# Two stores listed ahead of the last evictions, and twelve more idle products early on, in a fused mLSTM and feed-forward kernel

## The chip, the cores and the metric

One core of one Trainium2 chip runs the whole program as one launch. The metric is device time in microseconds (us). Smaller is better. Three runs of the kernel before gave 504.98, 501.16 and 502.6 us; the median is 502.6 us.

## The reference

The program computes two stages. The first is a gated recurrent attention (mLSTM) over 4 batches of 8 heads, 768 steps, head size 40. The second is a feed-forward layer with a rational activation over the 3072 resulting rows of 320 numbers.

```python
for t in range(S):
    m_new = np.maximum(f_gate[:, :, t] + m, i_gate[:, :, t])     # running maximum
    f_stab = np.exp(f_gate[:, :, t] + m - m_new)
    i_stab = np.exp(i_gate[:, :, t] - m_new)
    C = f_stab * C + i_stab * outer(vt, kt);  n = f_stab * n + i_stab * kt
    y[:, :, t] = sigmoid(o_gate[:, :, t]) * (C @ qt) / np.maximum(np.abs(n @ qt), 1.0)
h = x @ w_in                                  # x: y as 3072 x 320
P = a[0] + a[1] * h + a[2] * h**2 + a[3] * h**3
Q = 1.0 + np.abs(b[0]) * np.abs(h) + np.abs(b[1]) * h**2
out = (P / (Q + 1e-06)) @ w_out               # 3072 x 320
```

## The kernel before

**Work.** The recurrence is cut into chunks of 64 steps. A unit (`attention(u)`, u from 0 to 23) is one block of 128 steps of one batch; two units make one block of 256 rows for the feed-forward layer, so there are 12 such blocks. `feed_forward(n, i)` handles block n and hidden slice i (8 slices). Weights and activations are split into a high and a low part, and the parts are multiplied separately.

**Order.** Every operation is first put into a plan (`plan.add`) under a name such as `ev_11_7` (operation, block, slice). A second operation of the same name gets `.1`, a third `.2`. The text `ORDER` lists all names, and operations are issued in exactly that order. On one engine the listed order is therefore the order of execution. DMAs with the engine name `SP` are issued by SyncE in listed order; a DMA whose data is not ready holds up those behind it.

**Buffers.** `_Plan.issue` (line 122) chooses the physical buffer of a new tile when its first operation is issued: among the buffers of that kind it takes the one whose last user was issued the longest ago. A buffer with a user that has not been issued yet cannot be chosen. The framework then makes the new writer wait until the old readers of that buffer, stores included, have finished.

**The end.** The kind `ot` (line 1379), the staging tile of the output, has two buffers. The operation `ev` (`f_ev`, line 1378) copies a finished sum of 128 rows from PSUM into an `ot` tile; in the last block, `ev_11_7` is on ScalarE and `ev_11_7.1` on VectorE, and each also issues its own two stores, one on SyncE's queue and one on ScalarE's queue. For the earlier blocks the stores are an operation of their own, `ed` (`f_ed`, line 1395), with two stores on SyncE's queue. `ed_10_7` and `ed_10_7.1` store the two tiles of block 10.

```python
k = self.slot[tag] = min(range(bufs), key=free_since)       # line 132, _Plan.issue
...
ot = d["ot", t] = ring(fp, "ot", [P, DM], f"ot{n}_{t}")     # line 1379, f_ev
...
if last and not split:
    f_ed(t, (nc.scalar, nc.sync) if engine == "ACT" else (nc.sync, nc.scalar))
```

**The start.** `early()` (line 519) computes the running maximum and the exponentials of the first 256 steps on VectorE: the steps `early`, `early.1` and so on. `early.17` writes the exponentials into tile `g`; `early.18` (`turn`, line 551) is the only TensorE step of that list, a product with the identity that turns `g` (it writes tile `pe`). Behind it on TensorE stand `pf_0` (tile `fb`, 32 instructions), `pa_0` and `pa_1` (tile `pa`, 32 instructions each), which copy gate values across partitions, and `tk_0` (tile `kq`). ScalarE copies out what these write: `pc_0` and `pc_1` (tile `ab`), `ek_0` (tile `kT`), and after them prepares weights (`s2_o0`, `s0_o0`, and `o0_o1`, which writes tile `wo`). VectorE's `s1_o0` waits for `s0_o0`, its next step `o2_o1` reads what `o0_o1` wrote. GpSimd's `lx.1` is held until `o2_o1` is done, and the load `ogl_4` on SyncE's queue needs the buffer that `o2_o1` read last.

`busy()` (line 709) plans 90 operations `hot`: products of the identity with itself whose result nothing reads. Each is two instructions on TensorE. They are listed wherever TensorE would have nothing to do early in the program; the first 16 of them stand ahead of `early.18`. They read only the identity, so none of them waits for data of this stage.

Of the kernel before, what the change touches and what calls it, by code (L numbers as in the profile page):

```python
# [167 lines left out]
s0_o5.1 s2_o5 s2_i6 qa_0 hot.28 hot.29 hot.30 s1_o5.1 s0_o5 ow_0 tk_1 o0_o0 ke_1 s1_o5 ogl_2 ogl_0 s3_i6 s3_o5.1 u0_0
d1_0 ek_1 s3_o5 hot.31 hot.32 hot.33 hot.34 gate.7 gate.8 gate.9 gate.10 ogl_4 lq_1 tq_1 eq_1 lk_2 pf_2 u1_0 gate.11
qa_1 lv_1 o0_i4 o0_i6 kp_2 S_1 P_1 gate.12 P_1.1 pa_3 pc_3 ogl_5 sc_2 ogl_3 ow_1 u0_1 d1_1 gate.18 gate.13 gate.14  # L170
u1_1 gate.15 tk_2 ek_2 o2_i4 ogl_1 og_0 it_0 it_0.1 o2_i6 i1_0 gate.19 ke_2 hot.35 hot.36 hot.37 hot.38 hot.39 ab_0
ab_0.1 gate.16 raw_i0 lq_2 tq_2 rc_0 s0_i0 s2_i0 eq_2 o0_o5 s1_i0 s3_i0 o0_i0 g_0 x_0 g_0.1 hot.40 hot.41 hot.42
hot.43 raw_j1 s2_j1 qa_2 x_0.1 xd_0 S_2 P_2 P_2.1 lk_3 kp_3 o2_i0 pf_3 sc_3 o2_o0 s0_j1 s1_j1 raw_i1 xt_0 xh_0 xl_0
s2_i1 s0_i1 o2_o5 xh_0.1 xl_0.1 raw_i2 s0_i2 s2_i2 hot.44 hot.45 hot.46 s3_j1 ke_3 o0_j1 hot.47 hot.48 hot.49 hot.50
hot.51 hot.52 hot.53 hot.54 hot.55 f1_0_0 tk_3 ek_3 f1_0_0.1 ha_0_0 hot.56 hot.57 hot.58 s1_i1 lq_3 tq_3 gate.3 raw_o2
gate s3_i1 o0_i1 inverse squares gate.21 gate.17 hot.59 hot.60 hot.61 u_0_0 w_0_0 eq_3 o2_j1 s0_o2 hot.62 hot.63
hot.64 hot.65 hot.66 s1_i2 gate.20 s3_i2 s1_o2 p1_0_0 p3_0_0 S_3 gate.24 P_3 P_3.1 hot.67 hot.68 hot.69 hot.70 hot.71
hot.72 hot.73 s2_o2 s3_o2 o0_i2 raw_i3 s0_i3 s2_i3 lv_2 o2_i1 f1_0_1 f1_0_1.1 hot.74 hot.75 hot.76 hot.77 hot.78 s1_i3
s3_i3 y_0_0 r0_0_0 o2_j1.1 o2_i2 f1_0_2 f1_0_2.1 o0_i3 s0_o2.1 ha_0_1 u_0_1 p1_0_1 ha_0_2 u_0_2 w_0_1 w_0_2 lf_4 sc_4
gh_0_0 m_0_0 rm_0_0 s1_o2.1 p3_0_1 y_0_1 r0_0_1 gate.25 qa_3 hot.79 hot.80 hot.81 hot.82 hot.83 hot.84 hot.85 hot.86  # L180
hot.87 lk_4 gate.1 ow_2 u0_2 d1_2 gl_0_0 gh_0_1 m_0_1 rm_0_1 raw_o3 s2_o3 hot.88 hot.89 f2_0_0 lv_3 u1_2 s3_o2.1
p1_0_2 s0_o3.1 p3_0_2 ow_3 u0_3 s1_o3.1 raw_i5 ogl_6 d1_3 u1_3 o0_o2 it_1 it_1.1 i1_1 y_0_2 gl_0_1 s3_o3.1 s0_i5
f2_0_0.1 ab_1 ab_1.1 rc_1 raw_i7 o2_i3 lf_5 s0_i7 s2_i5 r0_0_2 kp_4 s1_i5 s1_i7 s2_i7 f1_0_3 f1_0_3.1 ha_0_3 g_1 g_1.1
f3_0_0 f3_0_0.1 o2_o2 p1_0_3 x_1 x_1.1 gh_0_2 xd_1 u_0_3 w_0_3 raw_o4 s0_o4.1 f2_0_1 f2_0_1.1 s3_i7 o0_i7 xt_1 xh_1
m_0_2 rm_0_2 p3_0_3 la_4 d0_4 lk_5 lq_4 xh_1.1 f3_0_1 f3_0_1.1 f2_0_2 f2_0_2.1 lq_5 s3_i5 o0_i5 tk_4 ke_4 kp_5 xl_1
xl_1.1 s1_o4.1 y_0_3 lv_4 s0_o4 gl_0_2 s2_o4 s3_o4.1 f1_1_0 f1_1_0.1 r0_0_3 gh_0_3 la_5 raw_o7 raw_o6 s1_o4 m_0_3 ek_4
s0_o3 s1_o3 ha_1_0 tq_4 eq_4 qa_4 s3_o3 s3_o4 f1_1_1 rm_0_3 gl_0_3 f1_1_1.1 f1_1_2 la_6 gate.33 lk_6 lv_5 p1_1_0
# [5 lines left out]
u_0_4 w_0_4 P_5.1 s1_o7 s3_o7 sc_6 gl_1_2 f1_0_5 ow_5 u0_5 kp_6 gate.31 ogl_9 la_7 gh_1_3 f1_0_5.1 ha_0_5 f1_0_6 lf_7
f1_0_6.1 s0_o6 s1_o6 u_0_5 d1_5 w_0_5 p1_0_4 p1_0_5 ha_0_6 f3_1_1.1 f2_1_2 f2_1_2.1 f3_1_2 m_1_3 s3_o6 u1_5 it_2
it_2.1 i1_2 gate.27 o0_o4 o2_o4 p3_0_4 rm_1_3 gl_1_3 ke_6 y_0_4 r0_0_4 gh_0_4 ab_2 ab_2.1 rc_2 g_2 g_2.1 tk_6 ek_6
p3_0_5 u_0_6 f3_1_2.1 f2_1_3 f2_1_3.1 m_0_4 rm_0_4 w_0_6 la_8 ogl_22 x_2 x_2.1 xd_2 y_0_5 r0_0_5 gh_0_5 f3_1_3
f3_1_3.1 tq_6 eq_6 lq_8 qa_6 gl_0_4 f1_0_7 f1_0_7.1 m_0_5 S_6 P_6 lk_8 p1_0_6 pe_1_3 pe_1_3.1 ha_0_7 s0_o6.1 p3_0_6
# [5 lines left out]
eq_7 f1_1_7 gate.22 gate.23 f1_1_7.1 f1_2_0 f1_2_0.1 gl_1_4 ha_1_7 ogl_11 ogl_7 gate.26 lv_7 lk_9 u_1_7 w_1_7 lf_8
ev_0_7.1 qa_7 gl_1_5 sc_7 ke_7 kp_8 ow_6 u0_6 d1_6 f2_1_4 f2_1_4.1 f3_1_4 lq_9 lk_10 ed_0_7 y_1_6 r0_1_6 p1_1_7 gh_1_6
ha_2_0 d0_7 u_2_0 og_6 S_7 P_7 P_7.1 p3_1_7 u1_6 sc_8 m_1_6 f3_1_4.1 f2_1_5 f2_1_5.1 f3_1_5 tk_8 ek_8 f3_1_5.1 f2_1_6
ow_7 u0_7 d1_7 w_2_0 p1_2_0 rm_1_6 gl_1_6 it_3 it_3.1 i1_3 tq_8 p3_2_0 u1_7 f2_1_6.1 f1_2_1 f3_1_6 f3_1_6.1 y_1_7
r0_1_7 gh_1_7 m_1_7 f1_2_1.1 d0_8 f2_1_7 ogl_14 f2_1_7.1 y_2_0 ab_3 ab_3.1 rc_3 g_3 g_3.1 r0_2_0 gh_2_0 rm_1_7 x_3
m_2_0 rm_2_0 gl_1_7 ha_2_1 p1_2_1 p3_2_1 u_2_1 eq_8 f1_2_2 f1_2_2.1 ha_2_2 p1_2_2 u_2_2 f3_1_7 x_3.1 gl_2_0 f3_1_7.1
ev_1_7 qa_8 ke_8 S_8 P_8 w_2_1 ogl_21 ed_0_7.1 p3_2_2 gate.29 ev_1_7.1 y_2_1 r0_2_1 gh_2_1 f1_2_3 kp_9 f1_2_3.1 ha_2_3
xd_3 xt_3 xh_3 w_2_2 m_2_1 y_2_2 u_2_3 r0_2_2 P_8.1 rm_2_1 w_2_3 f2_2_0 xl_3 f2_2_0.1 la_9 f3_2_0 f3_2_0.1 gh_2_2  # L210
p1_2_3 lq_10 p3_2_3 tk_9 ek_9 m_2_2 rm_2_2 f1_2_4 f1_2_4.1 f1_2_5 ha_2_4 gate.28 ogl_15 ogl_18 lf_9 sc_9 ke_9 kp_10
gl_2_1 y_2_3 r0_2_3 u_2_4 w_2_4 p1_2_4 xh_3.1 xl_3.1 gl_2_2 f1_2_5.1 ha_2_5 f2_2_1 f2_2_1.1 tq_9 eq_9 p1_2_5 f3_2_1
f3_2_1.1 f2_2_2 u_2_5 w_2_5 p3_2_4 gh_2_3 m_2_3 rm_2_3 y_2_4 r0_2_4 f2_2_2.1 f3_2_2 ogl_19 f3_2_2.1 f2_2_3 S_9 lk_11
lv_8 ogl_23 lv_9 lf_10 qa_9 P_9 P_9.1 gate.32 gh_2_4 m_2_4 ow_8 f1_2_6 f1_2_6.1 f1_2_7 f1_2_7.1 sc_10 u0_8 rm_2_4 d1_8
f2_2_3.1 gl_2_3 f3_2_3 f3_2_3.1 ha_2_6 u_2_6 w_2_6 p3_2_5 p1_2_6 u1_8 gl_2_4 ow_9 it_4 it_4.1 ed_1_7 y_2_5 d0_9 p3_2_6
u0_9 d1_9 u1_9 ha_2_7 u_2_7 w_2_7 r0_2_5 p1_2_7 gh_2_5 m_2_5 rm_2_5 p3_2_7 i1_4 ab_4 la_10 lq_11 lk_12 la_11 tk_10
ek_10 ke_10 ab_4.1 rc_4 g_4 kp_11 y_2_6 f2_2_4 f2_2_4.1 f1_3_0 gl_2_5 g_4.1 r0_2_6 gh_2_6 y_2_7 r0_2_7 m_2_6 rm_2_6
# [1308 lines left out]
```

## Time and profile before

| | |
|---|---|
| median of three runs | 502.6 us |
| profiled execution | 503.76 us, its span 502.0 us |
| mean granted TensorE clock | 0.985 of 2.4 GHz |
| TensorE busy | 479.1 us (95%) |
| VectorE, ScalarE, GpSimd busy | 418.6 us (83%), 400.0 us (80%), 380.2 us (76%) |
| chain that ended last, by engine | TensorE 82%, VectorE 9%, ScalarE 4%, DMA 2% |

The span is the time from the first to the last instruction of one profiled execution. "Busy" counts the time in which an engine executes something. The chain that ended last is followed back from the last instruction, at each step to what released it. A row with [3.77 <-DMA x] says that the engine sat idle for 3.77 us and that the DMA of x ended that wait. DMA issues are shown under SPq and ACTq, the queues of SyncE and ScalarE. The granted clock is given as a share of 2.4 GHz: 1.00 is that level, 0.50 is 1.2 GHz.

### The profile page before, as it was taken

Reading aid. Unit: us, or ns where it says so; the run is one execution under the profiler, and the core shown is the slowest. Engines: PE = TensorE matmul, PEld = TensorE weight load, DVE = VectorE, ACT = ScalarE, POOL = GpSimd, SP = SyncE. Lnnn points to the kernel's source line nnn. Section 1 sums busy time; section 2 is a strip of 40 time slices with the busy share of each in tenths; the row PEclk is TensorE's granted clock in tenths of the full one; section 3 lists DMA queues with packets and bytes.
Section 4 is the critical chain, followed back from the end, with each engine's and each line's share of the span. In section 5 each row is a group of like instructions: output and inputs, shape, how many; then the busy total and the mean of one; then the engine's idle time right before and its main releaser. Section 6 shows DMA issues by size and latency. Waiting matters only on the chain.

```text
span 502.0 us, 14204 instructions
## 1 busy us (share of the span) xinstructions
PE 479.1 (95%) x5631; PEld 462.8 (92%) x5631; DVE 418.6 (83%) x713; ACT 400.0 (80%) x696; POOL 380.2 (76%) x380
## 2 busy tenths in 40 slices
...
GB/s 200 187 165 235 209 172 158 103 79 69 118 120 123 94 93 27 150 84 24 66 69 79 68 82 2 74 80 64 2 117 27 21 76 3 37 5 2 14 0 47
DMA packets 119837, 42.01 MB, mean 84 GB/s; under 512 B 104274, under 2 KB 112530, under 8 KB 119762
## 3 DMA queue, kind: packets, MB, share of 16 engines
...
## 4 chain that ended last, share of the span: by engine, by line
PE 82%; DVE 9%; ACT 4%; DMA 2%; issue 1%; POOL 1%; SPq 1%; DVEq 0%; POOLq 0%; ACTq 0%
PE ph L34 34%; PE po L34 31%; PE kq L34 4%; PE y L34 4%; PE ow L34 3%; PE ps L34 3%; DVE w L34 2%; PE px L34 2%; DVE gH L34 1%; DVE gL L34 1%; PE hot L34 1%; DVE p L34 1%; PE pa L34 1%; PE fb L34 1%; DMA rawj<-in_moe_w_in_dram 1%
## 5 line engine op out<-in xcount | busy, mean ns | idle before, releaser
L34 PE MATMUL ph<-xk,wi 128*128 128x256 f32 x1152 | 169.8, 283 | 0.3 <-DVE na L34 0.3
L34 POOL TENSOR_TENSOR p<-p,w 128x512 f32<-128x512 f32 (+1 forms) x91 | 122.0, 1341 | 57.0 <-DVE w L34 52.5
L34 PEld LDWEIGHTS ph<-xk,wi 128*128 128x128 f32 x1152 | 148.1, 188 | 2.3 <-POOL wi L34 0.6
L34 POOL TENSOR_TENSOR w<-w,ha 128x512 f32<-128x512 f32 (+1 forms) x96 | 125.9, 1314 | 10.0 <-ACT w L34 6.1
L34 PE MATMUL po<-wo,gH 128*128 128x320 f32 x768 | 131.6, 310 | 0.0
L34 PEld LDWEIGHTS po<-wo,gH 128*128 128x128 f32 x768 | 115.4, 188 | 0.3
L34 DVE SCALAR_TENSOR_TENSOR w<-w,gH 128x512 f32<-128x512 f32 (+1 forms) x97 | 81.1, 837 | 4.2 <-DVE gH L34 0.5
L34 ACT ACTIVATE w<-ha,ba 128x512 f32<-128x512 f32 (+1 forms) x97 | 78.5, 811 | 6.0 <-POOL p L34 1.7
L34 DVE SCALAR_TENSOR_TENSOR gL<-p,ps,ph 128x512 fp32r<-128x512 f32 (+1 forms) x97 | 71.1, 734 | 14.3 <-POOL p L34 12.5
L34 DVE SCALAR_TENSOR_TENSOR gH<-p,ps,ph 128x512 fp32r<-128x512 f32 (+1 forms) x97 | 71.3, 735 | 12.6 <-ACT ph L34 9.1
L34 ACT ACTIVATE ph<-w,cd 128x512 f32<-128x512 f32 (+1 forms) x97 | 66.5, 687 | 16.3 <-DVE p L34 10.4
L34 ACT ACTIVATE ha<-ph 128x512 f32<-128x512 f32 (+1 forms) x97 | 57.5, 593 | 26.3 <-PE ph L34 25.6
L34 PE MATMUL po<-wo,gL 128*128 128x320 f32 x384 | 75.4, 312 | 0.8 <-DVE gL L34 0.6
L34 PE MATMUL ph<-xk,wj 128*128 128x256 f32 x384 | 75.3, 278 | 0.0
L34 DVE SCALAR_TENSOR_TENSOR p<-p,ps,ph 128x512 f32<-128x512 f32 (+1 forms) x97 | 70.7, 732 | 5.2 <-ACT p L34 5.2
L34 ACT ACTIVATE p<-ph,ps 128x512 f32<-128x512 f32 (+1 forms) x97 | 65.5, 678 | 0.0
L34 PEld LDWEIGHTS po<-wo,gL 128*128 128x128 f32 x384 | 59.1, 188 | 1.9 <-DVE gL L34 1.5
L34 PEld LDWEIGHTS ph<-xk,wj 128*128 128x128 f32 x384 | 58.1, 188 | 0.0
L34 ACT ACTIVATE ph<-ph 128x512 f32<-128x512 f32 (+1 forms) x97 | 56.3, 581 | 2.0
L34 PE MATMUL hot<-ident 128*128 128x128 f32 x180 | 26.0, 302 | 4.0 <-DVE flag_out L387 4.0
L34 PEld LDWEIGHTS hot<-ident 128*128 128x128 f32 x180 | 24.4, 215 | 4.2 <-issue 3.9
L34 DVE TENSOR_TENSOR pm<-ps,e 128x256 f32<-128x256 f32 x48 | 18.8, 416 | 8.5 <-PE ps L34 8.4
...
## 6 DMA issues: line engine op xcount, KB each, us to landing
...
vb<-in_v_dram SPq DMA_DIRECT2D x48, 80.0 KB, 3.1
out_dram<-ot SPq DMA_DIRECT2D x46, 80.0 KB, 2.3
...
```

The source lines that it names most:

```text
L34: made = fn(*args, **kwargs)
```

## The change

Two things are changed in the listed order. First, `HOT` goes from 90 to 102, and twelve of the products `hot` are put between `s2_i4` and `early.18`, so that 28 instead of 16 stand ahead of `early.18` on TensorE. The later ones keep their places and are only renumbered. Second, `ed_10_7.1`, the two stores of the second tile of block 10, stood as the last entry of the list, behind `ev_11_7.1`; it now stands right behind `ed_10_7`. Nothing is computed differently.

```diff
-HOT = 90
+HOT = 102
...
-raw_i4 s2_i4 early.18 s0_i4 early.19 early.20 o2_j0 pf_0 o2_j0.1 early.21 raw_i6 lk_0 kp_0 pa_0 s1_o1.1 lq_0 raw_o0
+raw_i4 s2_i4 hot.16 hot.17 hot.18 hot.19 hot.20 hot.21 hot.22 hot.23 hot.24 hot.25 hot.26 hot.27 early.18 s0_i4
...
-gl_11_0 ed_10_7 gl_11_1 f1_11_5 f1_11_5.1 f3_11_0 u_11_3 w_11_3 y_11_2 r0_11_2 gh_11_2 m_11_2 f3_11_0.1 f2_11_1
+gl_11_0 ed_10_7 ed_10_7.1 gl_11_1 f1_11_5 f1_11_5.1 f3_11_0 u_11_3 w_11_3 y_11_2 r0_11_2 gh_11_2 m_11_2 f3_11_0.1
...
-ev_11_7 ev_11_7.1 ed_10_7.1
+ev_11_7 ev_11_7.1
```

## Rows read from the trace of the kernel before

**Rows 1.** Chain of waits, last 12 us; columns: start us, us, what.

```profile
490.86 0.89 PE po L34 x5
...
491.76 0.54 ACT ot L34
...
492.32 2.52 DMA out_dram<-ot
...
495.02 0.55 DVE ot L34
```

**Rows 2.** Timeline from 465 us; start us, us, engine line op out<-in xcount [idle before <-releaser].

```profile
468.25 1.11 SPq L34 DMA_DIRECT2D out_dram<-ot  x2
...
495.02 0.55 DVE L34 TENSOR_SCALAR ot<-po,pa 128x320 f32<-128x320 f32 x1 [3.77 <-DMA out_dram<-ot]
...
495.60 0.47 SPq L34 DMA_DIRECT2D out_dram<-ot  x1
...
496.12 1.68 SPq L34 DMA_DIRECT2D out_dram<-ot  x2
```

**Rows 3.** SyncE's last two stores: duration ns min/median/max, first and last start; landing.

```profile
L34 SPq DMA_DIRECT2D out_dram<-ot x2: 587/812/1036, 496.1 to 497.2; - x2
...
DMA to landing us min/median/max: 2.7/2.7/2.7
```

**Rows 4.** DMA issues at 468.25, 492.32, 495.61 us; last column us from issue to landing.

```profile
out_dram<-ot SPq DMA_DIRECT2D x1, 80.0 KB, 2.0
...
out_dram<-ot SPq DMA_DIRECT2D x1, 80.0 KB, 2.3
...
out_dram<-ot ACTq DMA_DIRECT2D x1, 80.0 KB, 2.4
```

**Rows 5.** Timeline of TensorE's products, 0 to 27 us (columns as in rows 2).

```profile
3.96 6.12 PE L34 MATMUL hot<-ident 128*128 128x128 f32 x32 [3.96 <-DVE flag_out L387]
13.35 0.42 PE L34 MATMUL pe<-ident,g 128*64 128x128 f32 x1 [3.27 <-DVE gate_m L34]
13.71 1.98 PE L34 MATMUL fb<-g,ident 128*64 128x64 f32 x32
15.47 3.63 PE L34 MATMUL pa<-g,ident 128*64 128x64 f32 x64
...
20.35 1.15 PE L34 MATMUL pa<-g,ident 128*64 128x64 f32 x32 [0.45 <-ACT kT L34]
21.33 1.10 PE L34 MATMUL fb<-g,ident 128*64 128x64 f32 x32
...
24.31 2.72 PE L34 MATMUL hot<-ident 128*128 128x128 f32 x22
```

**Rows 6.** Stretches: length, busy us (count) of PE, PEld, DVE, ACT, POOL; PEclk, DMA share, GB/s.

```profile
9.00:10.10 1.10, 1.08 (x10) 0.89 (x8) 0.00 (x0) 1.09 (x2) 1.04 (x1) 1.00 0.81 244
...
12.00:12.30 0.30, 0.00 (x0) 0.00 (x0) 0.27 (x2) 0.30 (x1) 0.00 (x0) 0.83 1.05 289
...
18.80:19.20 0.40, 0.40 (x8) 0.28 (x5) 0.40 (x1) 0.06 (x1) 0.40 (x2) 0.72 1.67 202
...
75.00:87.50 12.50, 12.50 (x139) 12.01 (x138) 12.36 (x23) 12.27 (x22) 10.80 (x11) 1.00 0.70 165
```

**Rows 7.** Timeline of ScalarE, VectorE, SyncE's queue and GpSimd, 19 to 23 us.

```profile
19.14 0.59 ACT L34 COPY ab<-pa 128x512 f32<-128x512 f32 x1 [1.12 <-PE pa L34]
...
21.38 0.49 DVE L34 SCALAR_TENSOR_TENSOR lo0o<-rawo,lo0o 128x320 int32<-128x320 int32 x1 [1.31 <-ACT lo0o L34]
...
22.87 1.27 SPq L34 DMA_DIRECT2D og<-in_o_gate_dram  x2
22.99 0.40 POOL L34 TENSOR_TENSOR gate_x<-gate_f,gate_m 32x128 f32<-32x128 f32 x1 [2.29 <-DVE wo L34]
```

**Rows 8.** ScalarE's wait for the o gates, and landing of loads into `rawo`, 9 to 50 us.

```profile
36.37 1.36 ACT L34 ACTIVATE rawo<-rawo 128x640 f32<-128x640 f32 x2 [1.70 <-DMA rawo<-in_o_gate_dram]
...
DMA to landing us min/median/max: 2.9/5.2/8.0
```

More of the change, by code (lines that the diff above doesn't have):

```diff
@@ L168 @@
[L168 to L187, printed above, removed]
@@ L193 @@
[L193 to L197, printed above, removed]
@@ L203 @@
[L203 to L217, printed above, removed]
@@ L283 @@
[L283 to L285 removed]
+raw_i4 s2_i4 hot.16 hot.17 hot.18 hot.19 hot.20 hot.21 hot.22 hot.23 hot.24 hot.25 hot.26 hot.27 early.18 s0_i4
+early.19 early.20 o2_j0 pf_0 o2_j0.1 early.21 raw_i6 lk_0 kp_0 pa_0 s1_o1.1 lq_0 raw_o0 lk_1 s1_o1 s3_o1 s3_o1.1 pa_1
@@ new lines @@
+pc_0 pc_1 tk_0 ek_0 s2_o0 gate.5 gate.6 zero.2 sc_0 ke_0 s1_i4 s3_i4 s0_o0 s1_o0 o0_o1 o2_o1 s0_o0.1 hot.28 s1_o0.1
+pa_2 pc_2 lx.1 pf_1 tq_0 eq_0 raw_o5 s3_o0 kp_1 hot.29 hot.30 lx lx.3 li.1 li.3 lv_0 hot.31 S_0 P_0 P_0.1 li.2 li
+s0_i6 s1_i6 s3_o0.1 lx.2 hot.32 hot.33 hot.34 hot.35 hot.36 hot.37 hot.38 hot.39 sc_1 s0_o5.1 s2_o5 s2_i6 qa_0 hot.40
+hot.41 hot.42 s1_o5.1 s0_o5 ow_0 tk_1 o0_o0 ke_1 s1_o5 ogl_2 ogl_0 s3_i6 s3_o5.1 u0_0 d1_0 ek_1 s3_o5 hot.43 hot.44
+hot.45 hot.46 gate.7 gate.8 gate.9 gate.10 ogl_4 lq_1 tq_1 eq_1 lk_2 pf_2 u1_0 gate.11 qa_1 lv_1 o0_i4 o0_i6 kp_2 S_1
@@ new lines @@
+P_1 gate.12 P_1.1 pa_3 pc_3 ogl_5 sc_2 ogl_3 ow_1 u0_1 d1_1 gate.18 gate.13 gate.14 u1_1 gate.15 tk_2 ek_2 o2_i4 ogl_1
+og_0 it_0 it_0.1 o2_i6 i1_0 gate.19 ke_2 hot.47 hot.48 hot.49 hot.50 hot.51 ab_0 ab_0.1 gate.16 raw_i0 lq_2 tq_2 rc_0
+s0_i0 s2_i0 eq_2 o0_o5 s1_i0 s3_i0 o0_i0 g_0 x_0 g_0.1 hot.52 hot.53 hot.54 hot.55 raw_j1 s2_j1 qa_2 x_0.1 xd_0 S_2
+P_2 P_2.1 lk_3 kp_3 o2_i0 pf_3 sc_3 o2_o0 s0_j1 s1_j1 raw_i1 xt_0 xh_0 xl_0 s2_i1 s0_i1 o2_o5 xh_0.1 xl_0.1 raw_i2
+s0_i2 s2_i2 hot.56 hot.57 hot.58 s3_j1 ke_3 o0_j1 hot.59 hot.60 hot.61 hot.62 hot.63 hot.64 hot.65 hot.66 hot.67
@@ new lines @@
+f1_0_0 tk_3 ek_3 f1_0_0.1 ha_0_0 hot.68 hot.69 hot.70 s1_i1 lq_3 tq_3 gate.3 raw_o2 gate s3_i1 o0_i1 inverse squares
+gate.21 gate.17 hot.71 hot.72 hot.73 u_0_0 w_0_0 eq_3 o2_j1 s0_o2 hot.74 hot.75 hot.76 hot.77 hot.78 s1_i2 gate.20
+s3_i2 s1_o2 p1_0_0 p3_0_0 S_3 gate.24 P_3 P_3.1 hot.79 hot.80 hot.81 hot.82 hot.83 hot.84 hot.85 s2_o2 s3_o2 o0_i2
+raw_i3 s0_i3 s2_i3 lv_2 o2_i1 f1_0_1 f1_0_1.1 hot.86 hot.87 hot.88 hot.89 hot.90 s1_i3 s3_i3 y_0_0 r0_0_0 o2_j1.1
+o2_i2 f1_0_2 f1_0_2.1 o0_i3 s0_o2.1 ha_0_1 u_0_1 p1_0_1 ha_0_2 u_0_2 w_0_1 w_0_2 lf_4 sc_4 gh_0_0 m_0_0 rm_0_0 s1_o2.1
@@ new lines @@
+p3_0_1 y_0_1 r0_0_1 gate.25 qa_3 hot.91 hot.92 hot.93 hot.94 hot.95 hot.96 hot.97 hot.98 hot.99 lk_4 gate.1 ow_2 u0_2
+d1_2 gl_0_0 gh_0_1 m_0_1 rm_0_1 raw_o3 s2_o3 hot.100 hot.101 f2_0_0 lv_3 u1_2 s3_o2.1 p1_0_2 s0_o3.1 p3_0_2 ow_3 u0_3
+s1_o3.1 raw_i5 ogl_6 d1_3 u1_3 o0_o2 it_1 it_1.1 i1_1 y_0_2 gl_0_1 s3_o3.1 s0_i5 f2_0_0.1 ab_1 ab_1.1 rc_1 raw_i7
+o2_i3 lf_5 s0_i7 s2_i5 r0_0_2 kp_4 s1_i5 s1_i7 s2_i7 f1_0_3 f1_0_3.1 ha_0_3 g_1 g_1.1 f3_0_0 f3_0_0.1 o2_o2 p1_0_3 x_1
+x_1.1 gh_0_2 xd_1 u_0_3 w_0_3 raw_o4 s0_o4.1 f2_0_1 f2_0_1.1 s3_i7 o0_i7 xt_1 xh_1 m_0_2 rm_0_2 p3_0_3 la_4 d0_4 lk_5
@@ new lines @@
+lq_4 xh_1.1 f3_0_1 f3_0_1.1 f2_0_2 f2_0_2.1 lq_5 s3_i5 o0_i5 tk_4 ke_4 kp_5 xl_1 xl_1.1 s1_o4.1 y_0_3 lv_4 s0_o4
+gl_0_2 s2_o4 s3_o4.1 f1_1_0 f1_1_0.1 r0_0_3 gh_0_3 la_5 raw_o7 raw_o6 s1_o4 m_0_3 ek_4 s0_o3 s1_o3 ha_1_0 tq_4 eq_4
+qa_4 s3_o3 s3_o4 f1_1_1 rm_0_3 gl_0_3 f1_1_1.1 f1_1_2 la_6 gate.33 lk_6 lv_5 p1_1_0 p3_1_0 S_4 P_4 P_4.1 u_1_0 ha_1_1
+u_1_1 w_1_0 w_1_1 f1_1_2.1 o0_o3 o2_o3 tk_5 y_1_0 sc_5 ow_4 u0_4 d1_4 f1_1_3 ke_5 p1_1_1 p3_1_1 r0_1_0 gh_1_0 ek_5
+ha_1_2 s0_o7.1 s1_o7.1 s2_o7 f1_1_3.1 s3_o7.1 m_1_0 rm_1_0 o2_i7 f3_0_2 u1_4 f3_0_2.1 f2_0_3 p1_1_2 f2_0_3.1 y_1_1
@@ new lines @@
+lq_6 tq_5 lq_7 r0_1_1 lf_6 gh_1_1 m_1_1 u_1_2 w_1_2 gl_1_0 f3_0_3 f3_0_3.1 pe_0_3 ha_1_3 p3_1_2 pe_0_3.1 d0_5 o2_i5
+f1_0_4 f1_0_4.1 rm_1_1 eq_5 qa_5 gl_1_1 f2_1_0 f2_1_0.1 p1_1_3 p3_1_3 y_1_2 u_1_3 r0_1_2 s0_o7 gh_1_2 f3_1_0 f3_1_0.1
+lk_7 f2_1_1 S_5 w_1_3 P_5 m_1_2 rm_1_2 s2_o6 ogl_8 f2_1_1.1 y_1_3 f3_1_1 r0_1_3 ha_0_4 u_0_4 w_0_4 P_5.1 s1_o7 s3_o7
+sc_6 gl_1_2 f1_0_5 ow_5 u0_5 kp_6 gate.31 ogl_9 la_7 gh_1_3 f1_0_5.1 ha_0_5 f1_0_6 lf_7 f1_0_6.1 s0_o6 s1_o6 u_0_5
+d1_5 w_0_5 p1_0_4 p1_0_5 ha_0_6 f3_1_1.1 f2_1_2 f2_1_2.1 f3_1_2 m_1_3 s3_o6 u1_5 it_2 it_2.1 i1_2 gate.27 o0_o4 o2_o4
@@ new lines @@
+p3_0_4 rm_1_3 gl_1_3 ke_6 y_0_4 r0_0_4 gh_0_4 ab_2 ab_2.1 rc_2 g_2 g_2.1 tk_6 ek_6 p3_0_5 u_0_6 f3_1_2.1 f2_1_3
+f2_1_3.1 m_0_4 rm_0_4 w_0_6 la_8 ogl_22 x_2 x_2.1 xd_2 y_0_5 r0_0_5 gh_0_5 f3_1_3 f3_1_3.1 tq_6 eq_6 lq_8 qa_6 gl_0_4
+f1_0_7 f1_0_7.1 m_0_5 S_6 P_6 lk_8 p1_0_6 pe_1_3 pe_1_3.1 ha_0_7 s0_o6.1 p3_0_6 f2_0_4 s1_o6.1 P_6.1 s3_o6.1 p1_0_7
+rm_0_5 gl_0_5 p3_0_7 f2_0_4.1 u_0_7 w_0_7 f3_0_4 f3_0_4.1 f2_0_5 y_0_6 o0_o7 o2_o7 r0_0_6 gh_0_6 m_0_6 rm_0_6 xt_2
+y_0_7 xh_2 xl_2 gl_0_6 xh_2.1 kp_7 o0_o6 o2_o6 f1_1_4 f1_1_4.1 f1_1_5 ha_1_4 p1_1_4 p3_1_4 u_1_4 w_1_4 f1_1_5.1
@@ new lines @@
+f2_0_5.1 f3_0_5 tk_7 r0_0_7 f1_1_6 f1_1_6.1 f3_0_5.1 ha_1_5 u_1_5 p1_1_5 gh_0_7 m_0_7 xl_2.1 p3_1_5 rm_0_7 gl_0_7
+ogl_10 f2_0_6 f2_0_6.1 y_1_4 ha_1_6 r0_1_4 gh_1_4 u_1_6 f3_0_6 f3_0_6.1 f2_0_7 ogl_20 lv_6 f2_0_7.1 w_1_5 w_1_6 ek_7
+d0_6 f3_0_7 f3_0_7.1 ev_0_7 tq_7 m_1_4 rm_1_4 y_1_5 p1_1_6 p3_1_6 r0_1_5 gh_1_5 m_1_5 rm_1_5 eq_7 f1_1_7 gate.22
+gate.23 f1_1_7.1 f1_2_0 f1_2_0.1 gl_1_4 ha_1_7 ogl_11 ogl_7 gate.26 lv_7 lk_9 u_1_7 w_1_7 lf_8 ev_0_7.1 qa_7 gl_1_5
+sc_7 ke_7 kp_8 ow_6 u0_6 d1_6 f2_1_4 f2_1_4.1 f3_1_4 lq_9 lk_10 ed_0_7 y_1_6 r0_1_6 p1_1_7 gh_1_6 ha_2_0 d0_7 u_2_0
@@ new lines @@
+og_6 S_7 P_7 P_7.1 p3_1_7 u1_6 sc_8 m_1_6 f3_1_4.1 f2_1_5 f2_1_5.1 f3_1_5 tk_8 ek_8 f3_1_5.1 f2_1_6 ow_7 u0_7 d1_7
+w_2_0 p1_2_0 rm_1_6 gl_1_6 it_3 it_3.1 i1_3 tq_8 p3_2_0 u1_7 f2_1_6.1 f1_2_1 f3_1_6 f3_1_6.1 y_1_7 r0_1_7 gh_1_7 m_1_7
+f1_2_1.1 d0_8 f2_1_7 ogl_14 f2_1_7.1 y_2_0 ab_3 ab_3.1 rc_3 g_3 g_3.1 r0_2_0 gh_2_0 rm_1_7 x_3 m_2_0 rm_2_0 gl_1_7
+ha_2_1 p1_2_1 p3_2_1 u_2_1 eq_8 f1_2_2 f1_2_2.1 ha_2_2 p1_2_2 u_2_2 f3_1_7 x_3.1 gl_2_0 f3_1_7.1 ev_1_7 qa_8 ke_8 S_8
+P_8 w_2_1 ogl_21 ed_0_7.1 p3_2_2 gate.29 ev_1_7.1 y_2_1 r0_2_1 gh_2_1 f1_2_3 kp_9 f1_2_3.1 ha_2_3 xd_3 xt_3 xh_3 w_2_2
```

167 lines of the change are left out of this document (81 added, 86 removed).

## The prediction

> **What bounds the kernel now.** The page of the profile shows one dense middle and two thin ends, and the change touches only the ends. I read the chain of waits backwards from the end first. TensorE's last product ends near 491.75, ScalarE evicts one tile until 492.30, its stores take until 494.84, and only then does VectorE evict the other tile [rows 1]. VectorE had been idle for 3.77 us, and what ended this was a DMA that stores, not a product [rows 2]. An eviction reads PSUM and writes `ot`; it can wait for a store only if it shares that store's buffer. The code agrees: when `ev_11_7.1` is issued, the buffer of block 10's second tile still has an unissued user (`ed_10_7.1`, last in the list), so both last tiles get the same one. The reader is to see a serial tail: evict, store, evict, store, and two old stores behind.
>
> For the other end I read TensorE's timeline and then the granted clock by stretches. Sixteen products (32 instructions) run from 3.96 to 10.08; TensorE then idles 3.27 us until 13.35 for VectorE [rows 5]. The clock is 1.00 around 9 to 10 us, falls within 12.0 to 12.3 during that idle stretch (its mean there is 0.83), and is back only within 18.8 to 19.2 (mean 0.72) [rows 6]. In between it is 0.50, which is 1.2 instead of 2.4 GHz, and `pe`, `fb` and both `pa` run in it. In the middle, all engines are full: of 12.50 us from 75.0 on, TensorE is busy 12.50, VectorE 12.36, ScalarE 12.27 [rows 6]. A time by which the whole front moves should therefore pass through the middle unchanged.
>
> **The moved stores.** They now go out on SyncE behind `ed_10_7`, near 469.4, since the two before take 1.11 us from 468.25 [rows 2]. SyncE then has nothing to issue until the last evictions, so another 1.11 us there costs nothing; without that cover it would cost 1.11. At a landing of 2.0 us [rows 4] they are done before 473, long before their buffer is wanted again, so `ev_11_7.1` will find it free.
>
> **The end without the shared buffer.** VectorE can start with ScalarE at 491.76 and takes 0.55 [rows 1, 2], so both tiles are ready by 492.32. SyncE and ScalarE issue one store of each tile. The spacing of two stores on SyncE is 0.52 (495.60 to 496.12) [rows 2], so the last one goes out near 492.84. Before, the last one goes out at 497.2 and lands 2.7 later [rows 3], at 499.9; the span ends 2.1 after that, at 502.0, and I keep these 2.1. Landings are 2.0 for a lone pair on SyncE, 2.3 and 2.4 for stores that share the time with another queue's, 2.7 for the last two [rows 3, 4]. For four stores in half a microsecond I take 2.7, because the crowded stores at the end are the nearest row: last landing at 495.5, a gain of 4.4. The ends are 2.4, a gain of 4.7, and 3.0 (one more step of 0.3, as from 2.4 to 2.7), a gain of 4.1.
>
> The Trainium skill, "DMA: Bandwidth & Descriptors", section "Issuing engines are not separate DMA queues", speaks against a full gain: stores started by SyncE and ScalarE interleave on the same 16 engines, and a second queue saves only issue time. The rise from 2.0 to 2.7 in this trace agrees with it; by the rule alone the gain would be the 4.1.
>
> **The twelve products.** They are 24 instructions. At the full level 22 took 2.72 us [rows 5], 0.124 each, so 24 take 2.97. Behind 10.08 they end at 13.05, 0.30 before `pe` can start anyway. On TensorE they cost nothing as long as this idle stretch covers them. At the half level they take twice as long, 5.93, end at 16.01 and make `pe` 2.66 late. I take the full level, because ten records in the 1.1 us just before 10.1 are already dense [rows 6].
>
> What they can give: TensorE works until 13.05, beyond the point in 12.0 to 12.3 at which the clock fell [rows 6], and then idles 0.30 instead of 3.27 us. If the clock stays at 1.00, `fb` takes 1.10 instead of 1.98 and the two `pa` 2 x 1.15 instead of 3.63 [rows 5], together 0.88 + 1.33 = 2.2. So ScalarE's second copy of `pa` starts near 16.9 instead of 19.14, where it waited for TensorE [rows 7]. ScalarE's work behind it moves up as far. VectorE waited 1.31 for a product of that ScalarE chain, and was busy before, so VectorE gains 1.3 and not 2.2. GpSimd waited 2.29 for VectorE's next result `wo`, and SyncE's o-gate load at 22.87 goes out just after that same result [rows 7]; both inherit the 1.3. The loads queued behind it end in the o gates, for which ScalarE waited 1.70 at 36.37 [rows 8]. That is what all engines meet on, so I take 1.3 for the start. The ends are 2.2 (all of TensorE's gain) and 0 (loads land no earlier). What is late next is those loads. Nothing else is removed or added; renaming the later products has no cost.
>
> **The sum.** 4.4 + 1.3 = 5.7. Against the profiled execution, 503.76 - 5.7 = 498.1. That execution lies 1.16 above the median of the runs, so against the median it is 502.6 - 5.7 = **496.9**, a gain of 1.1%. A measurement of this kernel can tell about 1%, or 5.0 us, from no change.
>
> **The rivals.**
>
> *The start gives nothing.* The loads land when they did, because the DMA share in 12.0 to 12.3 and 18.8 to 19.2 is already above 1 [rows 6]; only the tail is gained: 502.6 - 4.4 = 498.2. For it: ScalarE does wait for a load at 36.37 [rows 8]. Against it: SyncE issued the load at 22.87 late for want of a buffer, not of bandwidth. Chance 0.22.
>
> *The products run at the half level.* The first 16 took 6.12 us, far over the 16 x 2 x 0.124 = 3.97 of the full level, so the early ones ran slowly although the clock is given as 1.00. If the rise comes later than 10 us, the twelve more hold up `pe` by as much as 2.66, and the start loses instead of gaining: 502.6 - 4.4 + 2.7 = 500.9. The rows near 9 to 10 us speak against it. Chance 0.08. By the Trainium skill, "TensorE: Matmul & The Clock Gate", section "The HAM clock gate", the point at which a starting engine reaches the full level varies from run to run; so this could show in some runs only. No run here shows how far it varies.
>
> *The buffer stays shared.* If `ev_11_7.1` still waits for a store, only the two trailing stores go: the last issue moves from 497.2 to about 495.6, a gain of 1.6, with the start 2.9, so 499.7. The selection in the code excludes it, as far as I can read it. Chance 0.03.
>
> *Slower: the loads collide.* Moving the front by 1.3 pushes loads into the crowded stretch up to 19.2 (DMA share 1.67 [rows 6]). Landings of the loads into `rawo` range from a median of 5.2 to 8.0 [rows 8], so a load that falls from the median to the longest costs 2.8. Three such on the path in a row are 8.4, which against the 5.7 makes 502.6 + 2.7 = 505.3. It decides from a loss of 5.7 on. Against it: the loads concerned go out after 21 us, and three in a row would have to be the longest. Chance 0.04; even then the loss is under 1%.
>
> **How the numbers follow.** The forecast has the remaining 0.63. Its own range comes from gains of 4.1 to 4.7 and of 0 to 2.2: 495.7 to 498.5. The three runs spread from 1.4 below to 2.4 above their median, so a new median may well lie 0.8 off. That opens the range to 494.9 below; above I reach to 499.8, which takes in the rival without a gain at the start and the shared buffer. The line of 1% is 497.6. The forecast lies 0.7 below it and holds under it some four times in five (0.50), the rival without a start gain one time in five (0.04): faster 0.54. Slower by over 1% would need more than 507.6; only a worse collision gives that, 0.03. The rest, 0.43, is within 1%.
>
> **What would show it.** Right: VectorE's last eviction begins within 0.1 us of ScalarE's and has no wait for `out_dram`; the last store goes out near 492.8 less the shift of the front, and the time from TensorE's last product to the end of the span falls from 10.3 to about 5.9. `hot` has 56 instructions ahead of `pe` and `pe` still starts at 13.35; the clock stays at 1.00 from 10 to 19 us, `pa` takes about 2.2, the idle 1.31 on VectorE is gone, and the o-gate load goes out near 21.5. Wrong: `pe` begins later than 13.4; the clock drops anyway; or the start of the first `ph` and of the last `po` do not move by what the load did, which would mean that the loads in between took the gain.

## The result, and the profile after

Five runs of the changed kernel gave 496.51 us (median; 495.61 to 497.47). The kernel before, run beside it, gave 501.16 (499.80 to 504.98). The ratio is **0.9898, with a 95% interval of 0.9852 to 0.9943**: about 5.1 us, or 1.0%, faster. Predicted were 496.9 and a gain of 5.7; the 496.9 was reckoned from 502.6, the median of the first three runs before, which lies 1.4 above the 501.16 of all five. The profiled execution took 495.61 us, its span is 493.8, the mean granted clock 0.997.

**The end.** First the changed kernel's timeline from 486.9 us (columns as in rows 2), then the four last stores with their landings, then the moved stores.

```profile
486.99 0.53 ACT L34 ACTIVATE ot<-po,pa 128x320 f32<-128x320 f32 x1 [3.43 <-PE po L34]
487.14 0.55 DVE L34 TENSOR_SCALAR ot<-po,pa 128x320 f32<-128x320 f32 x1 [0.66 <-PE po L34]
487.54 1.71 SPq L34 DMA_DIRECT2D out_dram<-ot  x2
487.55 2.00 ACTq L1402 DMA_DIRECT2D out_dram<-ot  x2
```

```profile
L34 SPq DMA_DIRECT2D out_dram<-ot x2: 467/809/1151, 487.5 to 488.1; - x2
L1402 ACTq DMA_DIRECT2D out_dram<-ot x2: 558/978/1399, 487.5 to 488.1; - x2
...
DMA to landing us min/median/max: 2.7/2.8/3.0
```

```profile
463.50 2.38 SPq L34 DMA_DIRECT2D out_dram<-ot  x4
```

VectorE's 3.77 us for a store [rows 2] are gone. It now waits for a product, as ScalarE does, and begins 0.15 us behind it. All four stores go out between 487.5 and 488.1, where before the last one went out 5.3 us behind TensorE's last product (497.2 against 491.87) [rows 3]. The block 10 stores, now four in a row, take 2.38 us of a queue with nothing else to do.

**The start.** TensorE's timeline of the changed kernel, to be laid beside [rows 5]:

```profile
3.95 9.10 PE L34 MATMUL hot<-ident 128*128 128x128 f32 x56 [3.95 <-DVE flag_out L388]
13.37 0.30 PE L34 MATMUL pe<-ident,g 128*64 128x128 f32 x1 [0.32 <-DVE gate_m L34]
13.71 1.15 PE L34 MATMUL fb<-g,ident 128*64 128x64 f32 x32
15.13 2.08 PE L34 MATMUL pa<-g,ident 128*64 128x64 f32 x64 [0.27 <-DVE lo1o L34]
...
19.45 1.10 PE L34 MATMUL fb<-g,ident 128*64 128x64 f32 x30
21.24 0.27 PE L34 MATMUL fb<-g,ident 128*64 128x64 f32 x2 [0.70 <-issue]
...
36.62 0.62 PE L34 MATMUL kq<-ident,qn 128*104 128x128 f32 x4 [0.28 <-DMA qn<-in_q_dram]
...
43.11 0.96 PE L34 MATMUL ph<-xk,wi 128*128 128x256 f32 x6
```

And the stretches (columns as in rows 6), and the other engines (as rows 7):

```profile
10.10:13.30 3.20, 2.95 (x27) 2.75 (x25) 2.88 (x9) 1.61 (x4) 0.23 (x2) 1.00 1.13 329
13.30:19.10 5.80, 4.97 (x124) 4.38 (x125) 5.62 (x14) 4.17 (x10) 3.37 (x4) 1.00 1.13 290
```

```profile
17.26 0.59 ACT L34 COPY ab<-pa 128x512 f32<-128x512 f32 x1 [0.35 <-PE pa L34]
...
19.99 0.49 DVE L34 SCALAR_TENSOR_TENSOR lo0o<-rawo,lo0o 128x320 int32<-128x320 int32 x1
...
21.43 1.28 SPq L34 DMA_DIRECT2D og<-in_o_gate_dram  x2
...
21.55 0.40 POOL L34 TENSOR_TENSOR gate_x<-gate_f,gate_m 32x128 f32<-32x128 f32 x1 [0.83 <-DVE wo L34]
```

The 56 instructions end 0.32 us before `pe`, which starts where it did. The clock stays at 1.00 through both stretches. `fb` takes 1.15 instead of 1.98, the two `pa` 2.08 instead of 3.63. VectorE's wait of 1.31 [rows 7] is gone, GpSimd's `gate_x` and the o-gate load come 1.44 earlier. New is a stop of 0.70 us on TensorE that no row of the profile explains (`<-issue`), 30 instructions into the second `fb`.

**Where the time went.** The three pieces of the span can be read from each profile: the start of the first `ph` (the first product of the feed-forward layer), from there to the end of TensorE's last product, and from that to the end of the span. The kernel before, in the timeline of 35 to 75 us:

```profile
39.96 1.06 PE L34 MATMUL kq<-ident,qn 128*104 128x128 f32 x4 [2.71 <-DVE lo0i L34]
...
47.78 0.95 PE L34 MATMUL ph<-xk,wi 128*128 128x256 f32 x6
```

Before: 47.78, 444.09 and 10.13. After: 43.11, 443.99 and 6.70. So this one pair says that the start gave 4.7 and the end 3.4, 8.1 together, while the runs say 5.1. The pair flatters the start: this execution of the kernel before was a late one (503.76 against a median of 501.16), and the experiments show where it lost.

### The profile page after: what moved, and what is told of

It reads as the page before. It is cut to its first block, busy times and chain, and to the rows that moved or that the text cites. A ratio compares the mean times of both kernels' runs of the same rounds, so it can differ in the third digit from the quotient of the medians.

```text
span 493.8 us, 14255 instructions
## 1 busy us (share of the span) xinstructions
PE 478.8 (97%) x5655; PEld 462.4 (94%) x5655; DVE 419.2 (85%) x713; ACT 400.0 (81%) x696; POOL 380.1 (77%) x380
## 4 chain that ended last, share of the span: by engine, by line
PE 84%; DVE 7%; ACT 3%; DMA 2%; issue 1%; POOL 1%; SPq 1%; DVEq 0%; POOLq 0%; ACTq 0%
PE ph L34 34%; PE po L34 31%; PE kq L34 4%; PE y L34 4%; PE ow L34 3%; PE ps L34 3%; DVE w L34 2%; PE px L34 2%; PE hot L34 2%; DMA qn<-in_q_dram 1%; DVE gH L34 1%; DVE gL L34 1%; DVE p L34 1%; PE pa L34 1%; PE fb L34 1%
## 5 line engine op out<-in xcount | busy, mean ns | idle before, releaser
L34 DVE SCALAR_TENSOR_TENSOR gH<-p,ps,ph 128x512 fp32r<-128x512 f32 (+1 forms) x97 | 71.4, 736 | 12.3 <-ACT ph L34 8.7
L34 PE MATMUL hot<-ident 128*128 128x128 f32 x204 | 28.1, 295 | 4.0 <-DVE flag_out L388 4.0
L34 PEld LDWEIGHTS hot<-ident 128*128 128x128 f32 x204 | 26.5, 209 | 4.2 <-issue 3.9
```

The source lines that it names most:

```text
L34: made = fn(*args, **kwargs)
```

## The experiments

Theories. **A**, the prediction's: the end gains because the two last tiles get different buffers and no store trails; the start gains about 1.3 because the clock stays up. **B**: the start gives nothing, since loads land when they did. For the end, a rival is that the freed queue does it and not the buffer. Each kernel with a ratio ran in five rounds beside the kernel before; e3, e5 and e6 ran once each, which hardly tells 1%, so they are read by their profiles alone.

### The two halves apart

e1 keeps the moved stores and drops the twelve products:

```diff
-HOT = 102
+HOT = 90
-raw_i4 s2_i4 hot.16 hot.17 ... hot.27 early.18 s0_i4
+raw_i4 s2_i4 early.18 s0_i4
```

> Only the two stores are moved; 90 products as before. My theory (the last two tiles no longer share a buffer): the last eviction on VectorE starts within 0.2 us of ScalarE's, its wait for the stores (3.77 us before) is gone, and TensorE's last product to the end of the span takes 6.5 to 6.9 us, as in the changed kernel (6.7), instead of 10.25. Time 3.5 us under the kernel before, 0.9930 of it; the clock still falls near 12.2 us and returns near 19. Rival (the stores of block 10 disturb the last block, or the tail's gain needs the earlier start): less than 2 us gained.

Measured: 498.00 us, ratio **0.9914 (0.9882 to 0.9946)**, which is 4.3 us of 502.6 (2.7 to 5.9). From its timelines of TensorE and VectorE:

```profile
15.49 2.48 PE L34 MATMUL pa<-g,ident 128*64 128x64 f32 x64
...
489.35 0.55 DVE L34 TENSOR_SCALAR ot<-po,pa 128x320 f32<-128x320 f32 x1 [0.66 <-PE po L34]
```

VectorE's last eviction waits 0.66 for a product and for no store; from TensorE's last product to the end of the span it is 6.49. The clock did fall behind the idle stretch, but came back early in this execution: 0.73 over 13.3 to 19.1, `pa` 2.48.

e2 does the reverse: twelve products, the stores back at the end of the list.

```diff
-gl_11_0 ed_10_7 ed_10_7.1 gl_11_1
+gl_11_0 ed_10_7 gl_11_1
-ev_11_7 ev_11_7.1
+ev_11_7 ev_11_7.1 ed_10_7.1
```

> Only the twelve products are added; the stores stand last as before. My theory (clock stays at the full level over 10 to 19 us): the pa products end near 17.1 instead of 19.1, VectorE's wait of 1.31 us is gone, the o-gate load goes out near 21.4 instead of 22.87, the first ph starts 1.0 to 1.7 us earlier than in a typical run before, and the whole takes 1.0 to 1.7 us less (0.9966 to 0.9980 of it); the tail of 10.25 us stays. Rival (the 4.7 us by which the first ph moved in the one profiled pair is all owed to the products): 4.7 us less, 0.9906. Rival (the loads take the gain): no difference.

Measured: 500.85 us, ratio **0.9973 (0.9940 to 1.0007)**: 1.4 us, from a loss of 0.35 to a gain of 3.0. One row each from e2's timelines of TensorE and VectorE:

```profile
15.26 2.08 PE L34 MATMUL pa<-g,ident 128*64 128x64 f32 x64 [0.27 <-DVE lo1o L34]
```

```profile
491.15 0.55 DVE L34 TENSOR_SCALAR ot<-po,pa 128x320 f32<-128x320 f32 x1 [3.85 <-DMA out_dram<-ot]
```

The clock is kept without the stores being moved, and the wait for the store is there without them. Within the intervals the two edits add up: 0.9914 x 0.9973 = 0.9887, against 0.9898 for both. By the ratios alone, B cannot be excluded.

e3 is the kernel before once more, and e9 the changed kernel once more.

> The kernel before once more, unchanged, for a second look at its start. If the products alone moved the first ph by 4.7 us, it starts at 47.8 again, with ScalarE's wait of 1.70 us for the o gates and TensorE's idle 2.7 us at 37 us. If those waits were a slow landing of one profiled execution, as I think, the first ph starts at 44.5 to 46.5 and the waits are shorter; the low clock of 12.2 to 19 us is there in either case, and the tail takes 10.2 us.

e3: 500.62 us. Low clock again (0.50 over 13.3 to 19.1, `pa` 3.63), and yet the first `ph` starts at 45.32 and not at 47.78. In the first profile TensorE had waited 2.71 before `kq` at 39.96 and fell to the low clock there once more (0.71 over 40 to 45); in e3 it waited 1.44 and stayed at 1.00. That is the chance part of the first pair.

> The change once more, on the same chip as e10, for a second profile and more runs. Stores alone gave 0.9914 and products alone 0.9973 of the kernel before; if the two parts add, the change lies at 0.988 to 0.990. The tail takes 6.4 to 6.8 us after TensorE's last product, pa ends near 17.2, and the first ph starts at 43.0 to 44.3 us, against 45.0 to 47.8 in the profiles without the twelve products.

e9: 496.16 us, ratio **0.9899 (0.9875 to 0.9924)**. Clock, `pe`, `fb` and `pa` as in the first profile of the change. The first `ph` at 44.60 is a little later than expected, the end piece of 6.08 a little shorter.

### The end: buffer or queue

e5 moves the stores, but makes both last tiles use one `ot` buffer:

```diff
-            ot = d["ot", t] = ring(fp, "ot", [P, DM], f"ot{n}_{t}")
+            ot = d["ot", t] = ring(fp, "ot", [P, DM], f"ot{n}_{t}", F32, 0 if last and not split else None)
```

> The two stores are moved as in the change (90 products), but the last two output tiles are put into the same buffer by hand. My theory (the shared buffer is the larger part of the tail, the two stores left behind the smaller): VectorE waits 3.6 to 3.9 us for the stores again, the last store goes out some 3.8 us after TensorE's last product, and the end of the span follows that product by 8.0 to 8.6 us, between the 10.0 of the kernel before and the 6.6 of the change. Rival (the two old stores at the very end were the whole loss): 6.6 us, as in the change.

```profile
490.37 3.81 SPq L34 DMA_DIRECT2D out_dram<-ot  x2
490.38 3.84 ACTq L1401 DMA_DIRECT2D out_dram<-ot  x2
493.14 0.55 DVE L34 TENSOR_SCALAR ot<-po,pa 128x320 f32<-128x320 f32 x1 [3.83 <-DMA out_dram<-ot]
```

e6 leaves the stores where they were, and gives the very last tile (`t == 1`, the one that VectorE evicts) the free buffer of another kind (`ha`):

```diff
         def f_ev(t, engine):
             ot = d["ot", t] = ring(fp, "ot", [P, DM], f"ot{n}_{t}")
+            if last and not split and t == 1:
+                ot = d["ot", t] = ring(fp, "ha", [P, W], f"ot{n}_{t}x", F32, 1 - plan.slot["ha"])[:, 0:DM]
```

> The order and the 90 products of the kernel before, but the very last tile is staged in a free buffer of another kind (the one of the tile ha). My theory: VectorE's last eviction follows ScalarE's within 0.2 us without a wait for a store; four stores then queue on SyncE and the last of them goes out some 3 us after TensorE's last product, so that the end follows by 7.6 to 8.5 us. Rival (the old order itself delays the eviction): the wait of 3.6 us stays and the tail takes 10 us.

```profile
489.46 0.55 DVE L34 TENSOR_SCALAR ot_1x<-po,pa 128x320 f32<-128x320 f32 x1 [0.66 <-PE po L34]
489.87 0.47 SPq L34 DMA_DIRECT2D out_dram<-ot  x1
...
490.43 0.81 SPq L34 DMA_DIRECT2D out_dram<-ot_1x  x1
...
491.29 1.32 SPq L34 DMA_DIRECT2D out_dram<-ot  x2
```

These rows settle it. With the queue free but the buffer shared, VectorE waits 3.83 as before, and the end piece is 8.57. With a buffer of its own and the old stores still trailing, the wait is gone and the end piece is 7.68, the old stores going out behind at 491.3 and 491.9. With both repaired it is 6.1 to 7.1, with neither 9.6 to 10.4. The buffer alone is worth about 2.4 of 10.1, the trailing stores alone 1.5, and together they give 3.5.

### The start: where it meets the loads

Behind 36 us TensorE waits in all profiles but e7 and e8 before the `kq` that turns the third load of `qn`: 0.28 us in the first profile of the change, 2.71 before, 2.73 in e1. That load takes 4.9 to 7.2 us to land (eleven profiles show it), and `kq` starts 0.13 to 0.14 us behind the landing in each of them, also where the row names VectorE's `lo0i`, which ends close by. Theory: the gain of the start is cut there. e7 lists this load ahead of the o-gate load `ogl_5`, in the changed kernel; e8 does the same in the kernel before.

```diff
-pa_3 pc_3 ogl_5 sc_2
+pa_3 pc_3 lq_2 ogl_5 sc_2
...
-gate.16 raw_i0 lq_2 tq_2
+gate.16 raw_i0 tq_2
```

> The changed kernel with one load listed earlier: the q load of unit 2, which in the five profiles so far goes out at 31.0 to 32.6 us and lands 5.6 to 7.2 later, and at whose landing TensorE then starts, is put ahead of the o-gate loads (near 26 us). My theory (this landing is where the start meets, and its length makes the runs differ): TensorE no longer waits for it, the first ph starts at 42.8 to 43.8 us whatever the landing, and the time is 0.3 to 1.5 us under the changed kernel, 0.987 to 0.9895 of the kernel before. Rival (the o gates, now 0.6 us later, take its place): same time as the change or 0.5 us over it.

> The kernel before with the same load listed earlier, and nothing else. If the q load's landing is what the start of the kernel before ends on, TensorE's idle 1.4 to 2.7 us near 37 us shrinks to under 1.2 (the o gates, 0.6 later, remain), the clock does not fall there, and the time is 1 to 2.5 us less (0.995 to 0.998). If it is the o gates or the weight pieces that end that wait, no change within 0.5 us.

e7: 496.54 us, ratio 0.9916 (0.9884 to 0.9948); e8: 501.82, ratio 1.0016 (0.9997 to 1.0035). In e7 the load goes out at 26.68 instead of 31.00, and `kq` does not wait for it. The first `ph` of e7 starts at 44.23, where 42.8 to 43.8 was expected. Nothing is gained in either. The waits of e8 between 30 and 45 us (engine and tile, what it waited for, us in total, times, longest) say why:

```profile
PE ps L34 <- ACT qT L34: 1.1, 1, 1.1
```

TensorE now waits one step later, for ScalarE's copy of that `kq`, and ScalarE stands behind its own late work on the o gates (it waited 0.69 for their load). In e7 TensorE waits 0.45 at the same place, and ScalarE, which makes that copy, shows no wait for the o gates there. So the theory of one late load fell: in e8 a second load, in e7 ScalarE's own work stands nearly as late as the first load, and taking that one away shows them.

### How many products

Four kernels with the moved stores and another number of extra products ahead of `early.18`, all edited as e1.

> The stores moved as in the change, and 24 instead of 12 products added. They run to about 13.05 + 2.8 = 15.9 us, so pe starts 2.5 us later than 13.35. My theory (the clock is the gain, a late pe the price): pa ends near 19.6 instead of 17.1, the gain at the start is lost again and the time lies 1 to 3 us over the changed kernel's 496.5, at 0.993 to 0.997 of the kernel before. Rival (more products keep the clock up later as well, or the start is bound by loads): within 0.5 us of the changed kernel.

> The stores moved as in the change, and 5 instead of 12 products added; they end near 11.3 us, and TensorE then idles 2.0 us before pe. If the clock falls in an idle stretch of any length, pa ends near 19.1 and the time is that of the stores alone (0.9914 of the kernel before). If five are enough to keep it, pa ends near 17.2 and the time is that of the change (0.988 to 0.990).

> The stores moved as in the change, 8 instead of 12 products added. In the four profiles with 12, TensorE stops for 0.7 to 1.5 us without a releaser two instructions before the end of the fb at 19.5 us, its 221st product; with 0, 5 and 24 it does not. If that stop belongs to a place in TensorE's own instruction stream, it now falls behind the fb, among the hot products at 21 us, or vanishes; the clock stays up (pa ends near 17.2), and the time is 0 to 1 us under the change (0.988 to 0.990 of the kernel before). If 8 are too few or the stop only shifts, the time equals that of the change or of 5 products (0.9927).

> The stores moved as in the change, 16 instead of 12 products added. They end near 13.9 us and make pe about 0.5 us late; a stop bound to the 221st product would fall on the 22nd instruction of the fb near 20 us. My theory: pa ends near 17.5, time 0 to 1 us over the change (0.990 to 0.992 of the kernel before), on the way to the 24 products' 0.9929. Rival (the place of the stop decides, not the late pe): no stop, and the time at or under the change.

| extra products | ratio (95%) | idle before `pe` | `pe` at | clock 13.3 to 19.1 | first `ph` |
|---|---|---|---|---|---|
| 0 (e1) | 0.9914 (0.9882 to 0.9946) | 2.89 | 13.38 | 0.73 | 45.32 |
| 5 (e10) | 0.9927 (0.9899 to 0.9955) | 1.94 | 13.38 | 1.00 | 44.57 |
| 8 (e11) | 0.9901 (0.9879 to 0.9922) | 2.20 | 13.40 | 0.71 | 46.21 |
| 12 (change) | 0.9898 (0.9852 to 0.9943) | 0.32 | 13.37 | 1.00 | 43.11 |
| 12 (e9) | 0.9899 (0.9875 to 0.9924) | 0.39 | 13.34 | 1.00 | 44.60 |
| 16 (e12) | 0.9944 (0.9919 to 0.9969) | 0 | 13.88 | 1.00 | 47.88 |
| 24 (e4) | 0.9929 (0.9899 to 0.9959) | 0 | 15.28 | 1.00 | 47.61 |

(The stop of which two of these texts speak is taken up at the end.) The intervals of all seven overlap. Overlap is not sameness, though: 16 lies 0.0043 over 8 and 0.0045 over 12 (e9), where chance would allow 0.0033 and 0.0035 if the two intervals of a pair are independent. The others cannot be told apart. No number beats twelve, and the profiles say what differs. With an idle stretch of about two us the clock held in one execution (e10) and fell in another (e11), there at 14.2 us, when TensorE was at work again. That e11's gap is longer than e10's with more products is because its early products ran faster: 48 instructions in 7.25 us, against 42 in 7.48, since their pace doubles at 7.4 us in e11 and at 9.3 in e10. With 16 and 24 the products themselves hold up `pe`, by 0.5 and 1.9; with 24 `pa` ends at 18.5, where 19.6 was expected. What held up the start in the profiled execution of e12 is something else. From its timelines of TensorE and of SyncE's queue:

```profile
15.13 2.08 PE L34 MATMUL pa<-g,ident 128*64 128x64 f32 x64
...
39.92 0.68 PE L34 MATMUL kq<-ident,qn 128*104 128x128 f32 x4 [3.94 <-DMA qn<-in_q_dram]
40.39 1.92 PE L34 MATMUL hot<-ident 128*128 128x128 f32 x8
```

```profile
16.68 6.21 SPq L34 DMA_DIRECT2D rawo<-in_o_gate_dram  x4
22.98 1.27 SPq L34 DMA_DIRECT2D og<-in_o_gate_dram  x2
```

TensorE runs `pa` at exactly the time of the changed kernel, but SyncE needs 6.21 us to issue four loads, where it needed 4.58 (from 16.32) in the changed kernel. The o-gate load goes out 1.55 later, the load of `qn` lands late, TensorE waits 3.94, and the clock falls just behind that wait: 0.66 over 40 to 45, eight `hot` in 1.92 instead of 1.06. Nothing in these rows ties that to the sixteen products: e5, without any extra product, needs 6.17 for the same four loads:

```profile
16.87 6.17 SPq L34 DMA_DIRECT2D rawo<-in_o_gate_dram  x4
```

The twelve runs of e12 spread from 495.39 to 500.97, and four of them are no slower than the changed kernel's 496.51; the profiled one is among the slowest. Whether sixteen products bring such executions about more often stays open.

## Why the prediction held, and which term was off

All 14 profiles split in three pieces at the two points named above. The middle piece, 444 us long, lies between 443.72 and 444.15 in every one. So the prediction's reading that the middle passes a shift on unchanged holds to 0.4 us, and the gain is that of the two ends:

| piece | without the edit | with it | gain | predicted |
|---|---|---|---|---|
| start: first `ph` at (mean; range) | 45.75 (44.97 to 47.78), 6 profiles | 43.98 (43.11 to 44.60), 4 profiles | 1.8 | 1.3 (0 to 2.2) |
| end: TensorE's last product to end of span | 10.06 (9.55 to 10.39), 4 profiles | 6.59 (6.08 to 7.07), 8 profiles | 3.5 | 4.4 (4.1 to 4.7) |

The start row compares no extra products (before, e1, e3, e5, e6, e8) with twelve (after, e2, e7, e9). The end row leaves out e5 and e6. 1.8 + 3.5 = 5.3, beside 5.1 from the ratio.

The total came out better than its parts. The end gave 0.9 less than forecast, outside its bounds, and the start by this table 0.5 more, so the two errors hide one another. That 496.9 and the measured 496.51 lie only 0.4 apart is luck besides: taken from the median of all five runs before, 501.16, a gain of 5.7 would have meant 495.5.

**The stores, point by point.** Moving them cost nothing: issued by 465.9 and landed 2.1 later, they are done 19 us before VectorE wants the buffer. VectorE's eviction was said to begin within 0.1 us of ScalarE's; it is 0.15. The 491.75 that the prediction read as the end of TensorE's last product is the end of the one that ScalarE waits for [rows 1]; VectorE waits for the last one, which ends at 491.87. The last store was said to go out at 492.84 less the shift. TensorE's last product ends at 487.10 instead of 491.87, a shift of 4.77, which makes 488.07; the row says 488.1. In the eight profiles it goes out 1.0 to 1.1 behind that product, before in four 4.9 to 5.5.

**The term that was mis-sized** is what follows the last store. The prediction kept the 2.7 of landing, because the last two stores of before were the nearest row, and kept 2.1 behind it. Reckoned with the longest landing of each profile, the landing is 2.7 to 3.6 (mean 3.1) in the eight with the new end, and was 2.5 to 2.7 (mean 2.55) in the four with the old one. What is left to the end of the span is 1.9 to 2.9 (mean 2.45), before 2.0 to 2.4 (mean 2.2); the last 1.3 of it are the program's closing semaphores and drains, 1.29 before and 1.34 after. For two of the old four, e2 and e8, the trace has no landing of the very last stores, and the longest of the earlier ones stands in. So of the 4.2 that the last store moved up, about 0.5 was lost in landing and 0.2 to 0.3 behind it; 3.5 remain, outside the bounds given. Two old stores on one queue were a poor stand-in for four on two queues: the second issue on each queue now takes 1.15 and 1.40 us (before 0.47 to 1.04 on SyncE).

The Trainium skill, "DMA: Bandwidth & Descriptors", section "Issuing engines are not separate DMA queues", was weighed in the prediction as speaking for the lower end of 4.1. The landings of 3.0 agree with its rule that stores started by two engines share the same DMA engines; the measured gain lies below even that end.

**The products, point by point.** 24 more instructions end at 13.05, as worked out, and `pe` starts at 13.37; in the other three profiles with twelve they end at 12.3 to 13.2, always ahead of `pe`. The clock holds at 1.00 in all four profiles with twelve. `pa` takes 2.08 (2.2 said), VectorE's 1.31 is gone, the o-gate load goes out at 21.43 (21.5 said). The size, 1.3, was right within what can be seen: 1.4 by the products alone, 0.8 as the difference between both edits and the stores alone, 1.8 by the first `ph`. What reaches the loads can be read apart from their landing: where the third load of `qn` stands at its old place in the list, it goes out at 30.9 to 31.5 with twelve products (three profiles, mean 31.1) and at 31.6 to 33.7 without (five, mean 32.7), 1.5 earlier. From there its landing (4.9 to 7.2) decides. Each of the six start points without products is later than each of the four with them, which speaks against the rival that the start gives nothing (chance 0.22); the ratio of e2 alone would not have excluded it. So the gain at the start is shown by the profiles and not by the times. That the engines meet on the loads is as the prediction said, but the load on which TensorE waits is the one of `qn`, and the prediction did not see that ScalarE stands nearly as late behind it (e7, e8).

**The other rivals.** That the products run at the half level: no profile with twelve shows it; 56 instructions take 8.3 to 9.3 us, and the slowest (e2) are done at 13.24, ahead of `pe`. The first products do run at half pace: in every profile they start 0.21 us apart, later ones 0.11. The step between the two lies at 7.4 to 9.8 us (8.8 before), in all 14 before the first 32 instructions are done. The trace's record of the clock begins only at that step, so the 1.00 that is printed for stretches ahead of it is no measurement. The pace of the first 32 varies with the step from run to run, from 5.46 (e11) to 6.59 us (e2); the Trainium skill, "TensorE: Matmul & The Clock Gate", section "The HAM clock gate", says that the point of the rise varies, and this agrees with it. That the buffer stays shared: it did not, and e5, built to be that rival, puts the last stores where it said, 3.3 us behind the first. That loads collide and make it slower: the landing of the `qn` load does vary by 2.3 us (4.9 to 7.2), with and without the change, and starts lie 2.8 apart in kernels without the edit. It comes from execution to execution and is no cost of the change that these profiles show.

By the chances given, faster by over 1% was at 0.54 and within 1% at 0.43. The ratio of 0.9898 lies on that line, with the interval on both sides of it.
